# Bucketed attention and a squared-ReLU layer on one core: the planner sees sums by bank, and the first and last microseconds are written anew

## The chip, the cores and the metric

One core of one Trainium2 chip runs the whole kernel. The metric is the device time of one execution in microseconds (us). The kernel is one launch, and its code for general inputs stands behind a branch that these inputs do not take.

## The reference

Attention over 4 batches of 8 heads, 768 tokens and 64 dims, in which a query sees only keys of its own bucket (six sign bits of a projection), and behind it a layer of 512 to 2048 to 512 with a squared ReLU.

```python
q_bits = (einsum('bhsd,dk->bhsk', q, proj) > 0)      # 6 bits, the same for k
mask = q_bucket[..., :, None] == k_bucket[..., None, :]
scores = where(mask, q @ k.T / sqrt(D), -1e9)
attn = softmax(scores)                               # over the keys
x = (attn @ v) as (B*S, 512)
h = maximum(x @ w_in, 0.0)
out = (h * h) @ w_out                                # (3072, 512) float32
```

## The kernel before

**Work.** The attention is cut into 192 units of 128 queries of one head. TensorE makes a unit's 128x768 scores in `pS` (a PSUM tile of two banks; every second one of the early units has a tile of three banks, called `pS2` in the code). VectorE copies them to `e` and takes their extreme (0.95 us a unit), ScalarE takes the exponential with its sum (0.93 us), and the weights are turned: for the first visits by TensorE (`pT`, copied to `aT` by ScalarE), later by a DMA transpose. A *visit* is one pair of heads and 384 queries; `av` multiplies the turned weights with the values (`pA`) and writes the result as two halves `xx`. Four visits fill the 512 features of a *group* of 384 tokens, of which there are eight. For each group `moe` (L849) runs the layer: sixteen times twelve matmuls into `pm`, ScalarE and VectorE make `g` from it, and nine matmuls add `g` times `w_out` into the group's sum `po`.

**The sum.** `po` (L890) is one PSUM tile of three banks, one bank for each 128 tokens, with one buffer: the next group's sum takes the same place. The last group uses `pS` and `pA` instead (L887). After the sixteenth part of a group, three copies `o<-po` (L916) bring the banks to SBUF, by ScalarE or VectorE (one of them always VectorE), and `out<-o` sends them.

**The start.** `run` (L474) fills small tiles, and `first` (L710) makes the buckets of the first pair of heads: `K` and `G` are loaded in two halves each, three float32 matmuls with `wide_pj` go into the three banks of one tile `pd` (L720), and VectorE makes the masks `MK`, `MK`, `MG` from them with the threshold `above` (in `marks`, from `unit_f`). `side_by_side` (L728) makes the first six units' scores from those.

**The order.** Nothing runs when it is written. `Program.add` (L176) records each operation with the operations that it depends on; `region` (L163) says which part of a tile an operation touches, and for a PSUM tile it always answers "all of it". `order` (L257) then plans all engines: a forward pass by rank, then up to `ROUNDS` times a backward pass that gives new priorities and a forward pass with them, and of all plans it keeps the one that is shortest by its own costs. `emit` (L426) issues the instructions of every engine in that order. The engines' real waits (semaphores) are set afterwards by the framework below, for the order that it is given; the planner's dependences only decide that order. In the first microseconds of a plan TensorE is idle, and `emit` puts matmuls on a tile of ones (`idle<-ones`) into the gaps: 0.6 of the planned gap, counted at 56 ns each (L439).

Of the kernel before, what the change touches and what calls it, by code (L numbers as in the profile page):

```python
# [12 lines left out]
BF16 = mybir.dt.bfloat16  # L13
F32 = mybir.dt.float32
# [3 lines left out]
AF = mybir.ActivationFunctionType  # L18
ALU = mybir.AluOpType
# [4 lines left out]
P = 128  # L24
B, H, S, D = 4, 8, 768, 64
NB = 6
HS = 384
# [14 lines left out]
PRICE = dict(pe=1, dve=3.57, act=0.3, pool=3.06, sp=0.43)  # L42
AHEAD, DELAY, LAG = 60, 2500, 1.0

ROUNDS, BEHIND = 4, 40000
LOADS = 0

PREP, STACKS, VALUES = -8, 0, 4
# [24 lines left out]
HS2 = 2.0**-9  # L73
QK_MAX, V_MAX, V_MIN, W_MAX, W_MIN, NORM_MAX = 16.0, 1.0, 2.0**-4, 2.0**15, 2.0, (1.38 * WS) ** 2

IDLE_FROM, IDLE_SHARE = 1000, 0.6

# [57 lines left out]
class Program:  # L137
# [24 lines left out]
    @staticmethod  # L162
    def region(view):  # L163
        ap, rec = view.ap, view.rec
        size = lambda dims: 1 + sum(st * (n - 1) for st, n in dims)
        if rec.kind == "dram":
            return 0, 1, ap.offset, ap.offset + size(ap.ap), 0, 0, 0
        p0, f0 = divmod(ap.offset, rec.row)
        if rec.kind == "psum":
            return 0, 1, 0, 1, 0, 0, 0  # L170

        (step, n), inner = ap.ap[1], size(ap.ap[2:])
        block = (step, f0 % step, f0 % step + inner) if n > 1 and f0 % step + inner <= step else (0, 0, 0)
        return (p0, p0 + ap.ap[0][1], f0, f0 + size(ap.ap[1:])) + block
# [251 lines left out]
    def emit(self):  # L426
        info = mybir.DependencyInfo(mybir.DependencyClass.NoSync, mybir.DependencyReason.DATA)
        last = {}
        def issue(q, ins):
            if q.key in last:  # L430
                self.tc.add_manual_dep(ins, last[q.key], info, reason="in order")
            last[q.key] = ins.name
        out = self.order()
        fill, end = {}, IDLE_FROM
        for i in out[: out.index(self.busy_from)]:
            o = self.ops[i]
            if o.queue is self.pe:
                if o.start > end + 300:
                    fill[i] = int((o.start - end) * IDLE_SHARE / 56)  # L439
                end = o.start + o.busy  # L440
        for i in out:
            o = self.ops[i]
            q = o.queue
            for _ in range(fill.get(i, 0) if self.idle[1].rec.tile is not None else 0):
                issue(q, q.engine.matmul(self.idle[0].real(), self.idle[1].real(), self.idle[1].real(), start=True, stop=True).ins)
            real = lambda x: x.real() if isinstance(x, View) else x
            if o.name == "matmuls":
                for args, kw in o.args:
                    ins = q.engine.matmul(*map(real, args), **kw).ins  # L449
                    issue(q, ins)  # L450
                continue
            ins = getattr(q.engine, o.name)(*map(real, o.args), **{k: real(x) for k, x in o.kw.items()}).ins  # L452
            issue(q, ins)
# [20 lines left out]
def run(ctx: ExitStack, tc, kq, v, proj2, w_in, w_out, consts, out, flag):  # L474
    fast = flag is not None
# [5 lines left out]
    pr = Program(tc)  # L481
    pe, dve, act, pool, sp = pr.pe, pr.dve, pr.act, pr.pool, pr.sp
    T, U = slice(0, D), slice(D, P)
# [3 lines left out]
    def send(out, x):  # L487
        sp.dma_start(out, x)
# [15 lines left out]
    def sb(shape, dtype, name, bufs=1, tag=None):  # L504
        return pr.tile(sbp, "sb", shape, dtype, name, bufs_of.get(tag or name, bufs), tag)

    def ps(shape, dtype, name, bufs=1, tag=None):
        return pr.tile(psp, "psum", shape, dtype, name, bufs, tag)
# [6 lines left out]
    cst = sb([P, 4], F32, "cst")  # L515
    if not fast:
        sp.dma_start(cst, consts[:, 0:4])
    pj = sb([P, 32], F32, "pj")
    dve.memset(pj, 0.0)
    ones = sb([P, P], BF16, "ones")  # L520
    dve.memset(ones, 1.0)
    pr.idle = ps([P, 512], F32, "idle", tag="pm")[:, 0:P], ones
    unit_f = sb([P, P], F32, "unit_f")
    if fast:
        pj0 = sb([P, 4 * NB], F32, "pj0")
        sp.dma_start(pj0[:, 0 : 3 * NB], proj2[:, NB : 4 * NB])
        sp.dma_start(unit_f, consts[:, 4 + 2 * P :])
        wide_pj = sb([P, P], F32, "wide_pj", tag="f")
        dve.memset(wide_pj, 0.0)
        given = pj0.rearrange("p (n c) -> p n c", c=2 * NB)[:, :, 0:NB]  # L530
        signed = pj[:, 0 : 4 * NB].rearrange("p (n c) -> p n c", c=NB)
        dve.tensor_scalar(signed[:, 0::3], given, 1.0, 1.0, ALU.mult, ALU.mult)
        dve.tensor_scalar(signed[:, 1:3], given, -1.0, 1.0, ALU.mult, ALU.mult)
        dve.tensor_scalar(wide_pj[:, 0 : 2 * NB], pj[:, 0 : 2 * NB], 1.0, 1.0, ALU.mult, ALU.mult)
        dve.tensor_scalar(wide_pj[:, D : D + 2 * NB], pj[:, 2 * NB : 4 * NB], -1.0, 1.0, ALU.mult, ALU.mult)
        marks = sb([P, 4], F32, "marks")
        above, balance, rest = (marks[:, n : n + 1] for n in range(3))
        for x, y, z in ((balance, 1.0, -SC), (rest, -1.0, 1.0 / SC)):
            dve.memset(x[T], y)
            dve.memset(x[U], z)  # L540
        dve.tensor_reduce(above, unit_f.rearrange("p (n c) -> p n c", c=32)[:, :, NB : 3 * NB], AX.XY, ALU.add)
        dve.tensor_scalar(above, above, -(2.0**-126), 1.0, ALU.mult, ALU.mult)
        maxes, sums = sb([P, UNITS], F32, "maxes"), sb([P, UNITS], F32, "sums")
    else:
        sp.dma_start(pj[:, 0 : 3 * NB], proj2[:, NB : 4 * NB])
        sgn_f = sb([P, 4 * P], F32, "sgn_f", tag="o")
        dve.memset(sgn_f, 0.0)
        for n in range(4):
            sp.dma_start(sgn_f[32 * n : 32 * n + 4 * NB, n * P : (n + 1) * P], consts[0 : 4 * NB, 4 : 4 + P])
        sgn = sb([P, 4 * P], BF16, "sgn")  # L550
        dve.tensor_copy(sgn, sgn_f)
        balance = cst[:, 2:3]
        thr = sb([P, 1], F32, "thr")
        dve.memset(thr, -(2.0**-80))
        sp.dma_start(unit_f, consts[:, 4 + 2 * P :])
        ident = sb([P, P], BF16, "ident")
        dve.tensor_copy(ident, unit_f)
# [152 lines left out]
    def first(hp, nq):  # L710

        K, G = [sb([P, n], F32, name, tag="VV") for name, n in (("K", S), ("G", nq))]
        for x, w in ((K, T), (G, U)):
            for odd, m in enumerate((T, U)):
                send(x[m], kq[0, 2 * hp + odd, w, 0 : x.shape[1]])
        MK, MG = sb([P, S], F16, "MK", tag="M"), sb([P, nq], F16, "MG", tag="Q")
        pd = ps([P, 3, 512], F32, "pd", tag="po")
        halves = K[:, 0:HS], K[:, HS:], G
        for n, x in enumerate(halves):
            pe.matmul(pd[:, n, 0 : x.shape[1]], wide_pj, x, start=True, stop=True)  # L720
        for n in range(2):
            dve.tensor_scalar(MK[:, n * HS : (n + 1) * HS], pd[:, n, 0:HS], above, 2.0**15, ALU.is_gt, ALU.mult)
        dve.tensor_scalar(MG, pd[:, 2, 0:nq], above, 2.0**15, ALU.is_le, ALU.mult)
        GS = sb([P, nq], F32, "GS", tag="L")
        move(GS, G, -SC)
        return K, GS, MK, MG

    def side_by_side(st, c0, i):  # L728

        K, G, MK, MG = st  # L730
        pr.rank = u - 1000
        both = [ps([P, 2, 512], F32, "pS"), ps([P, 3, 512], F32, "pS2", tag="po")]
        jobs = [[(n, x[:, j, 0:HS], a[m, c0 : c0 + P], bb[m, j * HS : (j + 1) * HS]) for x, m in zip(both, (T, U))] for n, (a, bb) in enumerate(((G, K), (MG, MK))) for j in range(2)]
        if not i:
            jobs = [[x[t]] for t in range(2) for x in jobs]
        for x in jobs:
            matmuls(*[y[1:] for y in x], start=x[0][0] == 0, stop=x[0][0] == 1)
        return both
# [110 lines left out]
    def moe(n, b, q0, nq):  # L849
        X = [xxs.pop((b, q0, cc)) for cc in range(NCC)]  # L850
        po, gs = None, {}
# [4 lines left out]
        for f in range(NF + 1):  # L856
# [23 lines left out]
            if f > 0:  # L880
                m = f - 1
# [23 lines left out]
                for t in range(nq // P):  # L905
                    r0 = b * S + q0 + t * P
                    if grouped and last:
                        if m == 3:
                            move(acc[:, t], po[t], back)
                        else:  # L910
                            dve.scalar_tensor_tensor(acc[:, t], po[t], back, acc[:, t], ALU.mult, ALU.add)
                        if m == NF - 1:
                            send(out[r0 : r0 + P], acc[:, t])
                    elif last:
                        o = sb([P, DM], F32, "o", tag="f")
                        move(o, po[t], back, (dve,) if fast and t == 1 else (act, dve, pool))  # L916
                        send(out[r0 : r0 + P], o)
            if n == 0 and f in (1, 5, 9):
                j = f // 4 + FIRST
                if j < 4:  # L920
# [161 lines left out]
```

## Time and profile before

| | us |
|---|---|
| runs shown: median of 3 (lowest, highest) | 809.61 (808.09, 810.79) |
| the profiled execution: its time | 811.04 |
| its span, from the first to the last instruction | 809.2 |
| TensorE busy in the span | 788.2 |
| ScalarE, VectorE, GpSimd busy | 643.3, 605.0, 85.4 |

In rows of the profile PE is TensorE, PEld its weight loads, DVE VectorE, ACT ScalarE, POOL GpSimd, SPq the queue of SyncE, which issues nearly all DMAs. A timeline row gives the start, the duration, engine, line, operation, output and inputs, the count, and in brackets how long the engine had been idle and what ended that. Records of matmuls that follow each other overlap: one of 512 columns has a record of 379 ns, but the next starts about 216 ns after it. The 809.2 us are the span; the time of the same execution is 1.8 us longer.

### The profile page before, as it was taken

What the parts mean: (1) busy time and instruction counts of PE and PEld (TensorE: products, weight loads), DVE (VectorE), ACT (ScalarE), POOL (GpSimd) and SP (SyncE); (2) the same over time, 40 slices, a digit from 0 to 9 for tenths busy, and PEclk for the clock granted to TensorE, in tenths of its full rate; (3) what the DMA queues carried; (4) which work ended last, traced back from release to release, by engine and by line L of the source; (5) the groups of instructions that cost most, each with busy time, mean ns of one, the idle gap of its engine ahead of it and who ended that gap; (6) DMA issues with size and microseconds to landing.
All of it is one profiled execution on the core that took longest, in us unless ns stands there. A gap on an engine that the chain in (4) does not pass through costs nothing.

```text
span 809.2 us, 14281 instructions
## 1 busy us (share of the span) xinstructions
PE 788.2 (97%) x4953; PEld 428.8 (53%) x4957; DVE 605.0 (75%) x1264; ACT 643.3 (79%) x1215; POOL 85.4 (11%) x168
## 2 busy tenths in 40 slices
PE   8887999999999999999999999999999999999996
PEld 5444555555555555555555555555555555555553
DVE  5998999999988989988988618898858761165111
ACT  4899999989988979988988738988767598863442
POOL 1555401200001101000000001110001000000000
PEclk9999999999999999999999999999999999999999
DMA  7777679999999999998989519989662289883001
GB/s 211 222 229 220 195 237 202 179 188 186 201 182 193 160 203 194 197 203 150 213 165 181 143 20 192 183 180 205 140 143 41 41 205 268 256 296 125 1 0 44
DMA packets 286240, 137.41 MB, mean 170 GB/s; under 512 B 259024, under 2 KB 266192, under 8 KB 286160
## 3 DMA queue, kind: packets, MB, share of 16 engines
q1 hardware_dynamic: 286160, 136.42, 75.3%
q8 instruction: 41, 0.67, 0.4%
q14 instruction: 39, 0.32, 0.1%
HBM read 56.36 MB, written 6.29 MB: 77 GB/s over the span
## 4 chain that ended last, share of the span: by engine, by line
PE 87%; DVE 2%; ACT 1%; issue 1%
PE pm L452 30%; PE po L452 27%; PE pS L452 16%; PE pA L449 11%; PE pA L452 1%; PE pd L449 1%; DVE e L452 1%; PE pT L452 1%; ACT o L452 0%; PE pt L452 0%; DVE win L452 0%; DVE f L452 0%; ACT e L452 0%; DVE VV L452 0%; ACT A L452 0%
## 5 line engine op out<-in xcount | busy, mean ns | idle before, releaser
L452 PE MATMUL pm<-xx,win 128*128 128x384 f16 x1536 | 306.2, 326 | 0.2 <-ACT g L452 0.2
L452 PE MATMUL po<-wo,g 128*128 128x512 f16 x1008 | 274.7, 379 | 0.2
L452 PEld LDWEIGHTS <-win 128*128 128x128 f16 x1536 | 149.4, 97 | 114.0 <-issue 3.8
L452 DVE TENSOR_SCALAR_CACHE_REDUCE e<-pS 128x768 f32<-128x768 f32 x192 | 182.8, 953 | 28.8 <-PE pS L452 26.4
L452 ACT ACTIVATE e<-e,maxes 128x768 f32<-128x768 f32 x192 | 178.6, 930 | 26.6 <-DVE e L452 24.5
L452 DVE SCALAR_TENSOR_TENSOR hl<-e,rv,hl 128x768 f16<-128x768 f32 x162 | 164.1, 1018 | 14.1 <-ACT hl L452 12.9
L452 PEld LDWEIGHTS <-g 128*128 128x128 f16 x1152 | 111.6, 97 | 118.4 <-issue 3.9
L452 ACT ACTIVATE hl<-e,rv 128x768 f16<-128x768 f32 x161 | 148.6, 925 | 9.8 <-DMA aT<-hl 8.5
L452 DVE SCALAR_TENSOR_TENSOR g<-g,g 128x384 f16<-128x384 f32 x112 | 61.9, 553 | 99.2 <-ACT g L452 98.3
L452 ACT ACTIVATE g<-g 128x384 f32<-128x384 f32 (+1 forms) x248 | 128.1, 518 | 9.7 <-PE po L452 6.3
L452 ACT ACTIVATE g<-pm 128x384 f32<-128x384 f32 x128 | 62.1, 485 | 83.8 <-PE pm L452 81.9
L452 PE MATMUL pS<-A,Q 128*128 128x384 f16 x372 | 94.4, 329 | 3.2 <-DVE e L452 2.9
L452 PE MATMUL pS<-L,M 76*128 76x384 f16 x372 | 95.2, 328 | 0.0
L452 POOL TENSOR_SCALAR rv<-sums 128x1 f32<-128x1 f32 x117 | 35.0, 300 | 475.1 <-ACT e L452 387.1
L449 PE MATMUL pA<-aT,VV 128*64 128x384 f16 x972 | 84.1, 327 | 0.0
L449 PEld LDWEIGHTS <-VV 128*64 128x64 f16 x972 | 52.8, 110 | 31.2 <-issue 9.3
L452 PEld LDWEIGHTS <-Q 128*128 128x128 f16 x372 | 34.4, 98 | 38.1 <-issue 12.8
L452 PEld LDWEIGHTS <-M 76*128 76x128 f16 x372 | 36.8, 99 | 23.9 <-issue 0.5
L452 PE MATMUL pT<-unit_f,e 128*128 128x128 f32 x180 | 30.1, 290 | 7.7 <-POOL e L452 4.2
L452 ACT ACTIVATION_READ_ACCUMULATOR e<-e,maxes 128x1 f32 x192 | 36.9, 192 | 0.0
L452 PE MATMUL pS<-wo,g 128*128 128x512 f16 x96 | 34.9, 379 | 0.0
L452 POOL TENSOR_SCALAR e<-e,rv 128x768 f32<-128x768 f32 x30 | 32.3, 1083 | 21.2 <-DVE rv L452 12.8
(85 smaller groups left out, 579.0 us busy)
## 6 DMA issues: line engine op xcount, KB each, us to landing
R<-kq SPq DMA_DIRECT2D x32, 384.0 KB
X<-kq SPq DMA_DIRECT2D x32, 384.0 KB
raw<-w_in SPq DMA_DIRECT2D x16, 511.8 KB
raw<-w_out SPq DMA_DIRECT2D x16, 511.8 KB
V<-vp SPq DMA_DIRECT2D x19, 384.0 KB
out<-o SPq DMA_DIRECT2D x24, 256.0 KB
X<-vp SPq DMA_DIRECT2D x16, 384.0 KB
Q<-A SPq DMA_DIRECT2D x32, 96.0 KB
```

The lines of the kernel that those rows point to most:

```text
L449: ins = q.engine.matmul(*map(real, args), **kw).ins
L452: ins = getattr(q.engine, o.name)(*map(real, o.args), **{k: real(x) for k, x in o.kw.items()}).ins
```

## The change

- `ROUNDS` is 8 and was 4: the planner makes up to nine plans and was making five.
- `region` gives for a PSUM tile the banks that an operation touches (`f0 // 512` and on), so the planner takes operations on different banks of one tile for independent.
- The idle matmuls of the first gap are counted at 112 ns instead of 56: 21 now, 46 before. Those of the second gap follow the new plan: 15 now, 20 before.
- `ones`, which the idle matmuls multiply, is filled by GpSimd as its first operation; it was VectorE's sixth kind of fill.
- A one-column exponential on `pj` (`table`) stands first on ScalarE, so the activation table is loaded there, and the two loads of `G` are issued by ScalarE's own queue behind it.
- The three first projections go to three tiles: `pd` in the places of `pA` and `misc`, and bank 2 of the first `pS2` (`other`), which the first pair of units then uses.
- The last copy of the program is put on ScalarE, and its `out<-o` is issued by ScalarE's queue.

```diff
-ROUNDS, BEHIND = 4, 40000
+ROUNDS, BEHIND = 8, 40000
...
-IDLE_FROM, IDLE_SHARE = 1000, 0.6
+IDLE_FROM, IDLE_COLD, IDLE_SHARE = 1000, 112, 0.6
+G_BY = "act"
...
         if rec.kind == "psum":
-            return 0, 1, 0, 1, 0, 0, 0
+            return 0, 1, f0 // 512, (f0 + size(ap.ap[1:]) + 511) // 512, 0, 0, 0
...
-                    fill[i] = int((o.start - end) * IDLE_SHARE / 56)
+                    fill[i] = int((o.start - end) * IDLE_SHARE / (56 if end > IDLE_FROM else IDLE_COLD))
...
+    ones = sb([P, P], BF16, "ones")
+    (pool if fast else dve).memset(ones, 1.0)
     pj = sb([P, 32], F32, "pj")
     dve.memset(pj, 0.0)
-    ones = sb([P, P], BF16, "ones")
-    dve.memset(ones, 1.0)
...
+        table = sb([P, 1], F32, "table")
+        act.activation(table, pj[:, 24:25], AF.Exp)
...
-        for x, w in ((K, T), (G, U)):
+        for x, w, by in ((K, T, sp), (G, U, getattr(pr, G_BY))):
             for odd, m in enumerate((T, U)):
-                send(x[m], kq[0, 2 * hp + odd, w, 0 : x.shape[1]])
+                by.dma_start(x[m], kq[0, 2 * hp + odd, w, 0 : x.shape[1]])
...
-        pd = ps([P, 3, 512], F32, "pd", tag="po")
+        other = ps([P, 3, 512], F32, "pS2", tag="po")
+        pd = [ps([P, 512], F32, "pd", tag=x) for x in ("pA", "misc")] + [other[:, 2]]
...
-                        move(o, po[t], back, (dve,) if fast and t == 1 else (act, dve, pool))
-                        send(out[r0 : r0 + P], o)
+                        end = fast and (b, q0 + nq) == (B - 1, S) and t == nq // P - 1
+                        move(o, po[t], back, (act,) if end else (dve,) if fast and t == 1 else (act, dve, pool))
+                        (act if end else sp).dma_start(out[r0 : r0 + P], o)
```

What that does to the order is shown at two places, with the semaphores that an instruction waits for in brackets (DMAHW: a DMA's, DVE, Activation, PE, Pool: that engine's).

The first place is the start on ScalarE. `GS` is the scaled `G`, `A` a copy of the loaded heads `R`, `e` a unit's exponential, `top` a step of the weights' conversion. Before:

```order
L452 ACT_TABLE_LOAD [waits DMAHW4_49]
L452 ACTIVATE GS<-G 128x384 [waits DMAHW3_49]
L452 ACTIVATE A<-R,marks 128x768 [waits DMAHW6_49,DVE_49]
L452 ACTIVATE A<-R,marks 128x768 [waits DMAHW7_49]
L452 ACTIVATE top_80<-raw 128x512 [waits DMAHW0_49,DVE_49]
L452 ACTIVATE e,sums<-e,maxes 128x768 [waits DVE_49]
L452 ACTIVATE top_83<-raw 128x512 [waits DMAHW1_49]
L452 ACTIVATE e,sums<-e,maxes 128x768 [waits DVE_49]
```

And now, to the second exponential:

```order
L453 ACT_TABLE_LOAD
L453 ACTIVATE table<-pj 128x1 [waits DVE_49]
L453 DMA G<-kq 64x384 x2
L453 ACTIVATE GS<-G 128x384 [waits DMAHW4_49,DMAHW2_49]
L453 ACTIVATE A<-R,marks 128x768 [waits DMAHW6_49,DVE_49]
L453 ACTIVATE A<-R,marks 128x768 [waits DMAHW7_49]
L453 ACTIVATE e,sums<-e,maxes 128x768 [waits DVE_49]
L453 ACTIVATE top_84<-raw 128x512 [waits DMAHW0_49]
L453 ACTIVATE top_89<-raw 128x512 [waits DMAHW1_49]
L453 ACTIVATE e,sums<-e,maxes 128x768 [waits DVE_49]
```

The table load no longer waits for `G`, two DMA issues are new on ScalarE, and both `top` steps now stand between the first and the second exponential.

The second place is TensorE at the end of the sixth group's sum; numbers tell the tiles apart, `po_7447` and `po_7556` are this group's sum, `pm` the next group's first part. Before, the last of the group's matmuls and what follows:

```order
L452 LDWEIGHTS g_8146
L452 MATMUL po_7447<-wo_627,g_8146 128x512
L452 LDWEIGHTS win_246
L452 MATMUL pm_8196<-xx_8153,win_246 128x384 [waits Activation_49]
L452 LDWEIGHTS win_246
```

Now, at the end of the same sum (`g_8180` and `g_8204` are its last two parts):

```order
L453 MATMUL po_7556<-wo_491,g_8204 128x512
L453 LDWEIGHTS g_8180
L453 MATMUL po_7556<-wo_491,g_8180 128x512 [waits Activation_49]
L453 LDWEIGHTS g_8204
L453 MATMUL po_7556<-wo_491,g_8204 128x512
L453 LDWEIGHTS g_8180
L453 MATMUL po_7556<-wo_491,g_8180 128x512
L453 LDWEIGHTS g_8204
L453 MATMUL po_7556<-wo_491,g_8204 128x512 [waits DVE_49]
L453 LDWEIGHTS g_8204
```

The copies `o<-po` of a bank that is ready have moved in between the group's last matmuls. The two matmuls with a wait write another bank of the same tile, and they wait until ScalarE's, then VectorE's copy has read its own. In the order before, no matmul of a group waited for a copy of that group; only the first matmul of the next group did, at two of the eight groups, 61 and 13 matmuls behind the last one. Now sixteen such matmuls wait, listed here with the engine whose copy they wait for and the number of other matmuls that stand between the matmul that lets the copy go and the one that waits for it ("next" is the first matmul of the following group):

| group | waits |
|---|---|
| 1 | ACT 4, DVE 40, next ACT 20 |
| 2 | ACT 0 |
| 3 | ACT 48, next ACT 24 |
| 4 | ACT 16, DVE 0, next ACT 12 |
| 5 | ACT 4, DVE 1 |
| 6 | ACT 0, DVE 0, next ACT 15 |
| 7 | ACT 12 |
| 8 (the last) | ACT 1 |

Ahead of the first `pm` matmul TensorE now has four more score matmuls (`pS`) and three more turns (`pT`); ScalarE has one more exponential, one more `aT` and one more `xx`, and two fewer `top` and three fewer halves of `w_out`. The number of matmuls in the program is the same but for the 30 idle ones.

More of the change, by code (lines that the diff above doesn't have):

```diff
@@ L712, in first @@
         K, G = [sb([P, n], F32, name, tag="VV") for name, n in (("K", S), ("G", nq))]
-        for x, w in ((K, T), (G, U)):
+        for x, w, by in ((K, T, sp), (G, U, getattr(pr, G_BY))):
             for odd, m in enumerate((T, U)):
-                send(x[m], kq[0, 2 * hp + odd, w, 0 : x.shape[1]])
+                by.dma_start(x[m], kq[0, 2 * hp + odd, w, 0 : x.shape[1]])
         MK, MG = sb([P, S], F16, "MK", tag="M"), sb([P, nq], F16, "MG", tag="Q")
-        pd = ps([P, 3, 512], F32, "pd", tag="po")
+        other = ps([P, 3, 512], F32, "pS2", tag="po")
+        pd = [ps([P, 512], F32, "pd", tag=x) for x in ("pA", "misc")] + [other[:, 2]]
         halves = K[:, 0:HS], K[:, HS:], G
         for n, x in enumerate(halves):
-            pe.matmul(pd[:, n, 0 : x.shape[1]], wide_pj, x, start=True, stop=True)
+            pe.matmul(pd[n][:, 0 : x.shape[1]], wide_pj, x, start=True, stop=True)
         for n in range(2):
-            dve.tensor_scalar(MK[:, n * HS : (n + 1) * HS], pd[:, n, 0:HS], above, 2.0**15, ALU.is_gt, ALU.mult)
-        dve.tensor_scalar(MG, pd[:, 2, 0:nq], above, 2.0**15, ALU.is_le, ALU.mult)
+            dve.tensor_scalar(MK[:, n * HS : (n + 1) * HS], pd[n][:, 0:HS], above, 2.0**15, ALU.is_gt, ALU.mult)
+        dve.tensor_scalar(MG, pd[2][:, 0:nq], above, 2.0**15, ALU.is_le, ALU.mult)
         GS = sb([P, nq], F32, "GS", tag="L")
         move(GS, G, -SC)
-        return K, GS, MK, MG
+        return K, GS, MK, MG, other
     def side_by_side(st, c0, i):
-        K, G, MK, MG = st
+        K, G, MK, MG, other = st
         pr.rank = u - 1000
-        both = [ps([P, 2, 512], F32, "pS"), ps([P, 3, 512], F32, "pS2", tag="po")]
+        both = [ps([P, 2, 512], F32, "pS"), ps([P, 3, 512], F32, "pS2", tag="po") if i else other]
         jobs = [[(n, x[:, j, 0:HS], a[m, c0 : c0 + P], bb[m, j * HS : (j + 1) * HS]) for x, m in zip(both, (T, U))] for n, (a, bb) in enumerate(((G, K), (MG, MK))) for j in range(2)]
```

## The prediction

> **What bounds the kernel now.** I read the page's first part and its chain, then the busy time by stages, then the timeline of the first microseconds.
>
> ```profile
> span 809.2 us, 14281 instructions
> PE 788.2 (97%) x4953; PEld 428.8 (53%) x4957; DVE 605.0 (75%) x1264; ACT 643.3 (79%) x1215; POOL 85.4 (11%) x168
> PE 87%; DVE 2%; ACT 1%; issue 1%
> ```
>
> TensorE is busy for 97% and carries 87% of the chain that ended last. That is an average; the stages tell more. I cut the span at the first exponential (14.76), at the layer's first matmul into `pm` (88.5) and at the end of the last matmul (802.21). Columns are TensorE, its weight loads, VectorE, ScalarE, GpSimd.
>
> ```profile
> L452 PE MATMUL pm<-xx,win x48: 322/326/327, 88.5 to 108.1; 128*128 128x384 f16 x48
> ...
> 0.00:14.76 14.76, 12.03 (x78) 8.32 (x79) 6.65 (x23) 4.35 (x6) 0.20 (x4) 1.00 0.69 211
> 14.76:88.50 73.74, 62.94 (x398) 35.97 (x395) 67.35 (x157) 70.70 (x147) 38.02 (x50) 0.95 0.73 218
> 88.50:802.21 713.71, 713.20 (x4483) 384.52 (x4485) 530.73 (x1086) 567.63 (x1064) 47.21 (x115) 1.00 0.77 164
> 802.21:809.20 6.99, 0.00 (x1) 0.00 (x0) 0.28 (x1) 0.60 (x1) 0.00 (x0) 0.87 0.34 122
> ```
>
> So there are three regimes. From 88.5 to 802.21 TensorE is idle for 0.5 of 713.7 us: whatever makes it wait there is added to the time, and whatever relieves the other engines is worth nothing. From 14.76 to 88.5 ScalarE is the full one (70.7 of 73.7). Before that it does little (4.35 of 14.76), so the start is worth what it moves ScalarE's first exponential.
>
> **The start.** What sets 14.76:
>
> ```profile
> 0.74 0.39 SPq L452 DMA_DIRECT2D pj<-proj  x1
> 1.18 1.21 SPq L452 DMA_DIRECT2D K<-kq  x2
> 2.43 1.24 SPq L452 DMA_DIRECT2D G<-kq  x2
> 2.73 5.09 PE L445 MATMUL idle<-ones 128*128 128x128 bf16 x46 [2.73 <-DVE ones L452]
> 6.00 1.28 ACT L452 ACT_TABLE_LOAD   x1 [6.00 <-DMA G<-kq]
> 7.61 2.03 PE L452 MATMUL pd<-K,wide_pj 128*128 128x384 f32 x4
> 9.47 0.81 PE L452 MATMUL pd<-G,wide_pj 128*128 128x384 f32 x2
> 10.32 0.62 DVE L452 TENSOR_SCALAR MK<-pd,marks 128x384 f16<-128x384 f32 x1 [3.82 <-PE pd L452]
> 11.91 1.94 DVE L452 SCALAR_TENSOR_TENSOR L<-A,marks,R 128x768 f16<-128x768 f16 x2
> 12.38 0.78 ACT L452 ACTIVATE top<-raw 128x512 f16<-128x512 bf16 x1 [2.61 <-DMA raw<-w_in]
> 13.76 0.95 DVE L452 TENSOR_SCALAR_CACHE_REDUCE e<-pS 128x768 f32<-128x768 f32 x1
> 14.46 1.29 PE L445 MATMUL idle<-ones 128*128 128x128 bf16 x20
> 14.76 0.94 ACT L452 ACTIVATE e<-e,maxes 128x768 f32<-128x768 f32 x1 [1.60 <-DVE e L452]
> 16.33 0.91 ACT L452 ACTIVATE e<-e,maxes 128x768 f32<-128x768 f32 x1
> ```
>
> The 46 idle matmuls (5.09 us, 111 ns each) hold the projections back to 7.61. `G`, issued by 3.67, is there at 6.00, 2.3 us later; `K`, issued by 2.39, should by the same lag be there at 4.7. The first mask waits for the third projection (10.28 to 10.32), and two `L` steps (1.94) stand ahead of the first `e`.
>
> After the change: 21 idle matmuls at 111 ns from about 1.1 (GpSimd fills `ones` first) end at 3.4 and hold nothing. `K`'s issues end at about 0.74+0.6+0.4+0.6 = 2.3, so it is there at 4.6. ScalarE's table load (1.28), the one-column step and two issues (1.24) from 0.8 end at 3.5, so `G` is there at 5.8, as before; it is needed only behind both `K` matmuls, so moving it gains nothing by itself, and the table load leaves ScalarE's path, which had slack there. What are the projections worth from 4.6?
>
> ```profile
> L452 PEld LDWEIGHTS pd<-K,wide_pj x4: 191/335/337, 7.5 to 8.8; 128*128 128x128 f32 x4
> L452 PEld LDWEIGHTS pd<-G,wide_pj x2: 190/190/190, 9.2 to 9.5; 128*128 128x128 f32 x2
> ```
>
> The same weight load takes 335 ns at first and 190 later, and the later 20 idle matmuls took 1.29 us (64 ns each) against 111 ns: TensorE ran at about half speed until some 8.5 us, 5.8 us after its first matmul, although the profile's own clock column says 1.00 there. With a shorter warm-up and a gap behind it I take half speed for the `K` matmuls (1.35 us each, half as fast as a `G` that takes about 0.7): 4.6 to 7.3, `G` to about 8.5, two score matmuls (1.4) and the mask's to 10.3, the first `e` at 10.5, the exponential at 11.5: 3.3 us earlier. The second one has both `top` steps ahead of it now (0.78 each): 11.5+1.1+1.6 = 14.2 for 16.33, 2.1 earlier. **I take -2.0**, the second's, since from there ScalarE is full. Bounds: 0 (a load or a cold clock is late next: `raw` ended an idle 2.61 us at 12.38) and -4.2 (full speed throughout). Of ScalarE's work up to 88.5, five steps of 0.5 to 0.8 us go and three of 0.5 to 1.1 come; I take nothing, within -1.5 and +0.5.
>
> **Work done earlier on TensorE.** Four score matmuls and three turns move ahead of 88.5, where TensorE has 10.8 us of idle time to hide them. Slots from the chain of waits:
>
> ```profile
> 101.17 0.37 PE pT L452 x3
> 112.67 1.95 PE pm L452 x12
> 119.22 1.94 PE po L452 x9
> ```
>
> 4 x 1.95/12 (384 columns, as `pS`) + 0.37 = **-1.0**.
>
> **The waits inside a sum.** The order of the changed kernel has sixteen matmuls that wait for a copy `o<-po`; the order before had two. The planner now thinks that a copy of one bank and a matmul into another are independent; the semaphores do not. That waits go by tile and not by bank is in the trace of before: the first `MK`, from bank 0 of `pd`, waited for the matmul into bank 2, and copies from different banks of one `po` wait for each other:
>
> ```profile
> DVE o L452 <- ACT o L452: 9.0, 6, 5.0
> L452 ACT ACTIVATE o<-po x14: 574/594/602, 193.6 to 743.3; 128x512 f32<-128x512 f32 x14
> L452 DVE TENSOR_SCALAR o<-po x7: 670/691/692, 194.8 to 742.6; 128x512 f32<-128x512 f32 x7
> L452 PE MATMUL po<-wo,g 128*128 128x512 f16 x1008 | 274.7, 379 | 0.2
> ...
> 801.83 0.38 PE L452 MATMUL pA<-wo,g 128*128 128x512 f16 x1
> 802.25 0.60 ACT L452 ACTIVATE o<-pA 128x512 f32<-128x512 f32 x1 [0.48 <-PE pA L452]
> 27.51 0.08 DVE L452 DVE_READ_ACCUMULATOR e<-pS 128x1 f32 x1
> 27.64 0.48 PE L452 MATMUL pS<-A,Q 128*128 128x384 f16 x2 [0.34 <-DVE e L452]
> ```
>
> One wait with nothing between: the matmul's record ends 379-216 = 0.16 us after its slot, the copy starts 0.04 later (802.21 to 802.25), takes 0.59 or 0.69, and TensorE goes on 0.05 after (27.59 to 27.64): 0.85 us for ScalarE, 0.94 for VectorE. By the table of waits: two of 0.85 and two of 0.94 with none between; one of 0.94-0.22 and, in the last group, one of 0.85-0.22 with one matmul between; two with four `pm` matmuls (0.65) between, 0.2 each. Sum 5.4. The other eight have 12 to 48 matmuls (2 us or more) as cover and cost nothing unless the copy is over a microsecond late. To this comes the copy's own wait: ScalarE is 80% and VectorE 74% busy in this stage, and a step found running has some 0.3 us left, so about 0.2 for each of eight: 1.6. **I take +7.0.** Bounds +4.1 (the 0.16 us by which a record's modelled end trails is not real, eight times) and +11 (copies stand behind steps that wait for loads themselves). Queued behind the waiting matmul is all of TensorE.
>
> The Trainium skill, PSUM — Partial Sum Buffer, its summary of rules for kernel authors, says that a matmul and a read of another bank may run at once and that semaphores go by bank. By that rule the term would be 0. The trace sides with the tile: the 9.0 us above.
>
> **The end.**
>
> ```profile
> 801.79 1.90 SPq L452 DMA_DIRECT2D out<-o  x3
> L452 SPq DMA_DIRECT2D out<-o x24: 332/432/1077, 232.4 to 803.3; - x24
> ```
>
> The last copy ended at 802.85, and SyncE issued its transfer at 803.3. ScalarE can issue at once: at best -0.45. But ScalarE's way to the end of the program now lies behind that issue of some 0.6: at worst +0.6. **I take -0.2.**
>
> **Sum.** -2.0 -1.0 +7.0 -0.2 = +3.8 on the profiled execution's 811.04. The median of the runs shown is 1.4 lower, 809.61; on it I forecast 813.4. A measurement of this kernel tells 0.3% (2.4 us) from no change.
>
> **Rivals.**
>
> *Balance.* The start gives its full 4.2 and the ramp 1.0, because `K` is there earlier and ScalarE's 3.0 us of idle time in it shrink; the waits cost their prompt 5.4. -5.2 -1.0 -0.2 +5.4 = -1.0: 808.6, no change. For it: the ramp is ScalarE's alone. Against: ScalarE's 70.7 us of work there stay.
>
> *The ramp runs away.* Faster. The planner's longer search finds an order in which the ramp to `pm` has no idle time on ScalarE (-3.0) and 1.5 us less work, with the start at -4.2, against waits at their low 4.1: -8.7 -1.0 -0.2 +4.1 = -5.8: 803.8. It decides from the point where the first `pm` matmul starts before 88.5-2.4-5.4+1.2 = 81.9. Against it: 70.7 us of work from a first exponential that is hardly before 14.8-4.2 = 10.6 end at 81.3 with no gap at all.
>
> *By bank.* The copies are no cost, by the skill's rule above or because TensorE comes to them late: -3.2, 806.4, faster. It decides where the waits cost under 0.8 in all. Against it: four of them have no matmul between.
>
> *Cold start.* TensorE stays at half speed into the first units: `G` and the first two units' scores (0.7, 1.4 and 0.3 more) put the first exponential at 13.9 instead of 11.5 and the second at about its old 16.3, and the shift is gone. 0 -1.0 +7.0 -0.2 = +5.8: 815.4. For it: it took 5.8 us of unbroken matmuls before, and now a gap from 3.4 to 4.6 lies in them. The Trainium skill, TensorE: Matmul & The Clock Gate, Part 1, has the clock doubled after a free-running window of about 3.4 us of sustained work; an estimate by it: a gap that spoils one window costs 3.4 us more at half speed, which would also take the shift. The trace agrees in kind, with 5.8 us until the change.
>
> **Chances.** Forecast 0.59 (0.51 slower, 0.08 within 0.3%), balance 0.16 (same), the ramp 0.09 and by bank 0.04 (faster), cold start 0.12 (slower). So faster 0.13, same 0.24, slower 0.63. The forecast's own range, with its bounds, is 810.5 to 817.5. To leave out no more than 2 in 10 the range reaches down to balance: 808.3 to 817.5.
>
> **What would show it.** Right: idle rows of PE ended by "ACT o" and "DVE o", about eight, 0.6 to 1.3 us each, where before there are none; TensorE idle from the first `pm` matmul to the last matmul at 6 to 9 us instead of 0.5; the first exponential at 11 to 12.5; the first `pm` matmul at 85.5 to 87.5; the first mask ahead of the third projection's end. Wrong: no idle time ended by `o`, or a first `pm` matmul before 83 or after 89, or a second stretch between 100 and 300 in which TensorE waits for ScalarE because five conversion steps were moved there.

## The result, and the profile after

| | before | after |
|---|---|---|
| median of six runs each, us | 810.68 (808.09 to 811.75) | 819.12 (816.97 to 821.71) |
| ratio to before | | 1.0107, 95% interval 1.008 to 1.0134 |
| profiled execution, us | 811.04, span 809.2 | 817.17, span 815.2 |

The change makes the kernel 8.4 us slower. The profiled execution of after is 2.0 us under the median of its runs and that of before 0.4 over its own, so the two profiles show 6.1 of it. First the page's head, and the stages cut as before: at the first exponential, the first matmul into `pm`, and the end of the last matmul.

```profile
span 815.2 us, 14274 instructions
PE 788.6 (97%) x4927; PEld 425.4 (52%) x4927; DVE 607.9 (75%) x1259; ACT 642.8 (79%) x1211; POOL 90.0 (11%) x178
```

```profile
L453 PE MATMUL pm<-xx,win x1536: 323/326/337, 87.7 to 803.6; 128*128 128x384 f16 x192
```

```profile
0.00:13.90 13.90, 9.81 (x45) 5.89 (x47) 6.01 (x21) 3.88 (x6) 0.41 (x5) 1.00 0.70 222
13.90:87.70 73.80, 64.63 (x409) 35.91 (x402) 69.63 (x159) 70.22 (x146) 36.37 (x48) 0.98 0.69 204
87.70:808.67 720.97, 714.18 (x4481) 383.63 (x4478) 531.67 (x1081) 568.15 (x1060) 53.23 (x125) 1.00 0.77 164
808.67:815.20 6.53, 0.00 (x0) 0.00 (x0) 0.57 (x1) 0.60 (x1) 0.00 (x0) 0.61 0.34 121
```

The first `pm` comes 0.8 us earlier than before, and the tail behind the last matmul is 0.46 shorter. The layer stage between them is 7.3 us longer (720.97 against 713.71), and TensorE is idle in it for 6.8 us instead of 0.5. What it waits for there (total, times, longest):

```profile
PE po L453 <- DVE o L453: 2.3, 3, 0.9
PE pS L453 <- DVE e L453: 1.5, 2, 0.9
PE po L453 <- ACT o L453: 1.4, 2, 0.7
PE pS L453 <- ACT o L453: 0.5, 1, 0.5
PE pm L453 <- DVE xx L453: 0.3, 1, 0.3
PE pS L453 <- ACT g L453: 0.3, 1, 0.3
PE pm L453 <- ACT g L453: 0.3, 1, 0.3
```

Six waits are for a copy `o` between two matmuls of one sum: 4.2 us in all, and none is longer than 0.9. Two of them stand 1.66 us apart in one sum:

```profile
677.83 0.81 PE L453 MATMUL po<-wo,g 128*128 128x512 f16 x3 [0.69 <-ACT o L453]
679.49 0.81 PE L453 MATMUL po<-wo,g 128*128 128x512 f16 x3 [0.85 <-DVE o L453]
```

The other 2.4 us, for `e`, `g` and `xx`, are new as well; in the same stage of before there is a single wait:

```profile
PE pm L452 <- ACT g L452: 0.2, 1, 0.2
```

These rows also add up to the longer stage: 6.3 us more idle time, eleven waits at 0.16 each for the modelled end of a matmul's record (1.8), less the 1.0 of work that moved ahead, make 7.1 of the 7.3. Now the start, in order of time (start, duration, what ended the idle time before it):

```profile
0.73 1.28 ACT L453 ACT_TABLE_LOAD   x1 [0.73 <-PEq L1080]
0.94 1.31 ACTq L453 DMA_DIRECT2D G<-kq  x2
0.99 2.42 PE L446 MATMUL idle<-ones 128*128 128x128 bf16 x21 [0.99 <-POOL ones L453]
2.00 0.49 SPq L453 DMA_DIRECT2D K<-kq  x1
4.82 0.25 DVE L453 TENSOR_SCALAR wide_pj<-pj 128x12 f32<-128x12 f32 x2
5.88 0.52 ACT L453 ACTIVATE GS<-G 128x384 f32<-128x384 f32 x1 [3.65 <-DMA G<-kq]
6.50 2.90 PE L453 MATMUL pd<-K,wide_pj 128*128 128x384 f32 x4 [3.09 <-DMA K<-kq]
8.16 0.62 DVE L453 TENSOR_SCALAR MK<-pd,marks 128x384 f16<-128x384 f32 x1 [1.20 <-PE pd L453]
9.20 1.49 PE L453 MATMUL pS<-G,wide_pj 128*128 128x384 f32 x2
13.90 0.94 ACT L453 ACTIVATE e<-e,maxes 128x768 f32<-128x768 f32 x1 [3.55 <-DVE e L453]
16.09 0.91 ACT L453 ACTIVATE e<-e,maxes 128x768 f32<-128x768 f32 x1
```

```profile
L453 PEld LDWEIGHTS pd<-K,wide_pj x4: 288/335/337, 6.5 to 7.9; 128*128 128x128 f32 x4
L453 PEld LDWEIGHTS pS<-G,wide_pj x2: 337/337/337, 8.6 to 9.2; 128*128 128x128 f32 x2
```

The idle matmuls end at 3.4 and the second half of `K` lands only at 6.5, so TensorE stands still for 3.1 us. The weight loads of the projections take 288 to 337 ns, all six of them (before, the last three took 190), and the projections of `K` and of `G` take 2.90 and 1.49 us for 2.03 and 0.81. `wide_pj`, which they multiply, is ready only at 5.1, because the load of `pj` now stands between the two halves of `K`. The first exponential gains 0.86, the second 0.24. At the end ScalarE issues the last transfer right behind its copy, in 0.36 us:

```profile
808.71 0.60 ACT L453 ACTIVATE o<-pA 128x512 f32<-128x512 f32 x1 [1.11 <-PE pA L453]
809.33 0.36 ACTq L453 DMA_DIRECT2D out<-o  x1
```

### The profile page after: what moved, and what is told of

Same layout as the page of the kernel before. It is cut to its first block, busy times and chain, and to the rows that moved or that the text cites. A ratio compares the mean times of both kernels' runs of the same rounds, so it can differ in the third digit from the quotient of the medians.

```text
span 815.2 us, 14274 instructions
## 1 busy us (share of the span) xinstructions
PE 788.6 (97%) x4927; PEld 425.4 (52%) x4927; DVE 607.9 (75%) x1259; ACT 642.8 (79%) x1211; POOL 90.0 (11%) x178
## 4 chain that ended last, share of the span: by engine, by line
PE 84%; ACT 2%; DMA 1%; issue 1%; DVE 1%; DVEq 0%
PE pm L453 29%; PE po L453 26%; PE pS L453 15%; PE pA L450 11%; PE pA L453 1%; DMA aT<-hl 1%; PE pd L450 1%; ACT hl L453 0%; PE pt L453 0%; ACT o L453 0%; ACT e L453 0%; DVE o L453 0%; ACT g L453 0%; PE pT L453 0%; DVE hl L453 0%
## 5 line engine op out<-in xcount | busy, mean ns | idle before, releaser
L453 PE MATMUL pm<-xx,win 128*128 128x384 f16 x1536 | 293.9, 326 | 0.6 <-DVE xx L453 0.3
L453 PE MATMUL po<-wo,g 128*128 128x512 f16 x1008 | 256.6, 379 | 3.8 <-DVE o L453 2.3
L453 ACT ACTIVATE g<-g 128x384 f32<-128x384 f32 (+1 forms) x242 | 124.9, 517 | 6.7 <-PE po L453 3.0
L453 PE MATMUL pS<-A,Q 128*128 128x384 f16 x372 | 92.4, 328 | 4.8 <-DVE e L453 3.5
L453 PE MATMUL pS<-L,M 76*128 76x384 f16 x372 | 92.3, 327 | 0.5 <-DVE L L453 0.4
L453 POOL TENSOR_SCALAR rv<-sums 128x1 f32<-128x1 f32 x126 | 39.7, 315 | 432.9 <-ACT e L453 398.7
L453 PEld LDWEIGHTS <-Q 128*128 128x128 f16 x372 | 34.7, 98 | 40.5 <-issue 15.1
L453 DVE SCALAR_TENSOR_TENSOR L<-A,marks,R 128x768 f16<-128x768 f16 x32 | 32.1, 1012 | 4.0 <-ACT A L453 3.8
```

## The experiments

Two suspects: the waits for copies between the matmuls of a sum, and a TensorE that stays at half speed because of the gap at the start. The rivals are the new order as such, the eight rounds of planning, and losses that only move to another wait. "Whole tile" is the kernel before's rule for dependences in PSUM, "by bank" the changed one's. The ratios are to the kernel before on the same chip; before itself had medians of 810.4 to 811.1 there. So two kernels are compared by their ratios, where 0.0010 is 0.8 us; after's loss is 8.7 us by its ratio and 8.4 by the medians.

One number helps to compare traces with different orders: how far TensorE is **behind** at a time, that is the time less the slots of the matmuls started by then (median distance of starts in before: 162 ns for 384 columns in f16, 216 for 512, 82 for `pA`, 110 for a turn; idle matmuls count nothing). A few missing records make it good to about 1 us. It is worked out from one profile of each kernel, like the time from which TensorE runs fast (the first entry in the trace's list of granted clocks, where the weight loads turn from slow to fast too) and the waits of TensorE from 100 us on. The time of the profiled execution stands beside the median: those of e1, e2, e5 and e12 are 1.5 to 2.3 us over it, those of after, e3 and e7 1.5 to 2.0 under.

| kernel | median us | ratio | profiled us | fast from | first exp. | behind at 100 | lost from 100 to the end | waits for `o` / others |
|---|---|---|---|---|---|---|---|---|
| before | 810.7 | 1 | 811.0 | 8.7 | 14.8 | 30.7 | 17.6 | 0 / 0.2 |
| after | 819.1 | 1.0107 | 817.2 | 11.4 | 13.9 | 29.7 | 24.2 | 4.2 / 1.8 |
| e1 whole tile | 815.7 | 1.0057 | 817.2 | 18.9 | 15.0 | 32.0 | 21.2 | 0 / 2.4 |
| e2 copies behind | 818.5 | 1.0089 | 820.8 | 19.3 | 15.0 | 32.7 | 23.4 | 0 / 5.0 |
| e3 bank alone | 815.0 | 1.0049 | 813.5 | 7.9 | 13.5 | 29.0 | 21.1 | 1.6 / 1.5 |
| e4 eight rounds | 810.4 | 0.9999 | 810.3 | 8.5 | 14.7 | 28.3 | 19.1 | 0.8 / 0.6 |
| e5 third bank | 813.4 | 1.0043 | 815.4 | 15.1 | 14.9 | 31.3 | 20.8 | 1.0 / 2.6 |
| e6 long warm-up | 815.4 | 1.0071 | 814.9 | 4.2 | 11.2 | 27.7 | 23.9 | 4.2 / 1.7 |
| e7 short warm-up | 810.3 | 0.9997 | 808.8 | 7.1 | 12.9 | 29.0 | 16.5 | 0 / 0.2 |
| e8 whole tile, warm | 812.4 | 1.0027 | 813.2 | 6.8 | 11.6 | 28.5 | 21.0 | 0 / 2.5 |
| e9 the same, `G` by SyncE | 811.7 | 1.0008 | 812.5 | 7.0 | 11.4 | 26.2 | 23.3 | 0 / 3.3 |
| e10 third bank, warm | 811.4 | 1.0011 | 811.7 | 5.8 | 11.8 | 27.9 | 21.2 | 1.0 / 2.5 |
| e11 eight rounds, short | 809.4 | 0.9982 | 808.4 | 6.8 | 12.7 | 26.5 | 20.0 | 0.8 / 0.8 |
| e12 all cures | 814.3 | 1.0048 | 816.1 | 6.5 | 13.2 | 32.1 | 21.9 | 1.2 / 2.0 |

### The waits inside a sum

**Whole tile again** (e1). All else of the change stays.

```diff
-            return 0, 1, f0 // 512, (f0 + size(ap.ap[1:]) + 511) // 512, 0, 0, 0
+            return 0, 1, 0, 1, 0, 0, 0
```

> The changed kernel with dependences in PSUM by the whole tile again; all its other edits stay (start, table load, G by ScalarE's queue, eight rounds, last transfer). Its order has no copy `o` between the matmuls of a sum, only three waits of a next group with 13 to 44 matmuls as cover. Theory (the waits inside the sums, 5.2 us in the trace of the changed kernel, and the 3.2 us of waits for `e` and `g` that came with them, are the loss): idle rows ended by `o` gone, 819.1 - 5.2 = 813.9 if the 3.2 us belong to something else, 819.1 - 8.4 = 810.7 if they go too. Rival A (the start, eight rounds or the order as such cost it): 817 or more, with TensorE's idle time in the layer stage still 6 us or more.

815.68 us, ratio 1.0057 (1.0042 to 1.0072). All waits for `o` are gone, and about half of the loss came off (4.1 of 8.7 us by the ratios): between theory and rival. It isn't a clean test, for the start differs too: the profiled execution, the slowest of the six, had its first exponential at 15.0 and TensorE 2.3 us further behind at 100 than that of after.

**Copies behind the sum** (e2). The planned order stays; a copy and its transfer that stood between two matmuls of a sum are emitted behind its last one.

```diff
         out = self.order()
+        out = self.behind_sums(out)
```

> The changed kernel's own order, with the copies `o` (and their transfers) that stood between the matmuls of a sum moved behind the last matmul of that sum; nothing else moves, and the dependences stay by bank. Theory: the six waits for `o` go, 5.2 us: 813.9; if the 3.2 us of waits for `e` and `g` were made by the copies in their way, 810.7. Rival A (the order as such): 817 or more. Rival B (a copy that comes later only holds the next group's first matmul, with 12 to 20 matmuls as cover): waits for `o` of the same sum at the groups' beginnings, 818.

818.48 us, ratio 1.0089 (1.0072 to 1.0106): no gain is clear of the noise, since after's interval is 1.0080 to 1.0134. No wait for `o` is left, not even at a next group, so rival B is out; but the waits for `e` went from 1.5 to 3.6 us (from 90 us on):

```profile
PE pS L472 <- DVE e L472: 3.6, 9, 0.5
PE pS L472 <- ACT g L472: 0.8, 1, 0.8
PE pm L472 <- ACT g L472: 0.5, 2, 0.3
```

Part of that comes from the copies put off: one stands ahead of a unit's step `e` on VectorE, and TensorE waits for that step.

```profile
203.01 0.69 DVE L472 TENSOR_SCALAR o<-po 128x512 f32<-128x512 f32 x1 [0.82 <-ACT o L472]
203.62 0.95 DVE L472 TENSOR_SCALAR_CACHE_REDUCE e<-pS 128x768 f32<-128x768 f32 x1
204.63 0.50 PE L472 MATMUL pS<-A,Q 128*128 128x384 f16 x2 [0.43 <-DVE e L472]
```

The same is seen at 504 and 613 us, with one or two steps between, 1.1 us in all three. But three of the nine waits for `e` (1.4 us) lie at 126 to 143 us, ahead of the first copy, so the rest stays open. This isn't the cure, and it says little of the cause, since the profiled start was as cold as in e1.

**The third bank of `po` a tile of its own** (e5). Every row of the order stays; only which tile the third bank belongs to is changed, and so what a semaphore covers.

```diff
+        if kind == "psum" and tuple(shape[1:]) == (3, 512):
+            make = lambda: Banks(pool.tile([shape[0], 2, 512], dtype, name=name, tag="po", bufs=1), lambda: pool.tile([shape[0], 512], dtype, name=name, tag="third", bufs=1))
```

> The changed kernel with its order unchanged in every row, but the third bank of `po` a tile of its own, so that a matmul into it no longer waits for a copy out of the other two. Of the six waits for `o` in the trace of the changed kernel one stays inside a sum of `po` (0.6 us, one matmul between) and the one in the last group (0.47); gone are the others, 3.1 us of visible idle time and 0.16 us more each by the modelled ends. Theory (these waits are a loss of their own, and go by tile): 819.1 - 3.8 = 815.3. Rival A (a wait that is taken away comes back as a wait for `e`, as when the copies were moved behind the sums, where 5.2 us of waits went and 0.6 came off the time): 818.5, with TensorE's waits for `e` up from 1.5 us to 4 or more.

813.43 us, ratio 1.0043 (1.0027 to 1.0059): 5.2 us less than after by the ratios (give or take 2.5), where 3.8 was expected, and although its profiled start was colder (31.3 behind at 100 for 29.7). Where after waited twice in the sum at 677 us, one wait is left:

```profile
677.69 1.24 PE L467 MATMUL po<-wo,g 128*128 128x512 f16 x5 [0.47 <-ACT o L467]
```

```profile
PE pS L467 <- DVE e L467: 2.6, 5, 1.0
PE pS L467 <- ACT o L467: 0.5, 1, 0.5
PE po L467 <- ACT o L467: 0.5, 1, 0.5
```

So the waits are by tile and not by bank, and they cost what they show: in the profiles 3.2 us of them less gave 3.4 of the loss from 100 us on (24.2 to 20.8). Some came back as waits for `e` (1.5 to 2.6 us), the rival's way on a small scale.

**By bank alone, and eight rounds alone,** on the kernel before (e3, e4).

```diff
-            return 0, 1, 0, 1, 0, 0, 0
+            return 0, 1, f0 // 512, (f0 + size(ap.ap[1:]) + 511) // 512, 0, 0, 0
```

> The kernel before with dependences by bank alone (four rounds, old start, old end). Its order has one copy with no matmul between it and the waiting one, one by VectorE with four, and one in the last group with one matmul between. Theory, prompt: 0.85 + 0.3 + 0.64 = +1.8 on 810.7: 812.5, the start and the first `pm` as before. Rival A (an order planned by bank loses 8 us whatever stands in the sums): 816 or more. Rival by bank (the copies cost nothing): 810.7, no idle row ended by `o`.

815.04 us, ratio 1.0049 (1.0032 to 1.0067). The three waits for `o` are there at 1.6 us (forecast 1.8), but the loss is 4: 1.5 us more are for `e`, `g` and `xx`, which the order before does not have.

```diff
-ROUNDS, BEHIND = 4, 40000
+ROUNDS, BEHIND = 8, 40000
```

> The kernel before with eight rounds of planning alone. Its order has no copy inside a sum and six waits of a next group, of which two have ten matmuls (1.6 us) as cover and the copy some 1.4 us of ScalarE's work. Theory: no change, 810.7 within 1.5. Rival A (the longer search lands in a worse order by itself): 814 or more.

810.38 us, ratio 0.9999 (0.9987 to 1.0012), as expected: by the profiles it is 2.4 us further on at 100 and loses 1.5 of it by the end. Its ramp also has no stretch at half clock, where that of before has 6.8 us of it (76.9 to 83.7, the 0.95 in the clock column of its ramp). How much of the 2.4 us that is, no run tells.

### The clock at the start

**The long warm-up** (e6). The order stays; 43 idle matmuls instead of 21.

```diff
-IDLE_FROM, IDLE_COLD, IDLE_SHARE = 1000, 112, 0.6
+IDLE_FROM, IDLE_COLD, IDLE_SHARE = 1000, 56, 0.6
```

> The changed kernel with twice as many idle matmuls ahead of the first projection (about 42 for 21, 0.99 to 5.7 us), its order otherwise the same. Cold start (TensorE, let go idle from 3.4 to 6.5 us, stays at half speed until 11.5 to 17, and the first exponentials come late): weight loads of `K` at 335 ns only up to about 7 us, 190 behind, the first exponential at about 11.9 instead of 13.9 to 15.0, the first `pm` some 2 to 3 us earlier, 819.1 - 3 = 816.1. Rival (the clock at the start is not worth anything, since ScalarE or the loads hold the ramp): first exponential earlier, but 819 as before.

815.43 us, ratio 1.0071 (1.0057 to 1.0085): 2.9 us less by the ratios (give or take 2.5; 3.7 by the medians), as expected. `K` still lands only at 6.1 and the gap is 1.1 us, but TensorE comes to it at full speed; the idle matmuls turned fast at 4.2 already (43 took 4.06 us, at 0.115 each they would have taken 4.9):

```profile
0.99 4.06 PE L446 MATMUL idle<-ones 128*128 128x128 bf16 x43 [0.99 <-POOL ones L453]
6.12 0.94 PEld L453 LDWEIGHTS pd<-K,wide_pj 128*128 128x128 f32 x4 [1.25 <-issue]
6.16 1.53 PE L453 MATMUL pd<-K,wide_pj 128*128 128x384 f32 x4 [1.10 <-DMA K<-kq]
8.26 1.70 PE L450 MATMUL pS<-K,GS 64*128 64x384 f32 x6
11.18 0.94 ACT L453 ACTIVATE e<-e,maxes 128x768 f32<-128x768 f32 x1 [0.66 <-DVE e L453]
13.42 0.91 ACT L453 ACTIVATE e<-e,maxes 128x768 f32<-128x768 f32 x1
```

The same six score matmuls in e1, with the short warm-up, and the loads of all 24 such matmuls (least, median, most), there and in e6:

```profile
10.43 3.09 PE L450 MATMUL pS<-K,GS 64*128 64x384 f32 x6
15.04 0.94 ACT L453 ACTIVATE e<-e,maxes 128x768 f32<-128x768 f32 x1 [5.96 <-DVE e L453]
...
L450 PEld LDWEIGHTS pS<-K,GS x24: 182/236/334, 10.4 to 23.2; 64*128 64x128 f32 x24
```

```profile
L450 PEld LDWEIGHTS pS<-K,GS x24: 182/186/187, 8.3 to 18.5; 64*128 64x128 f32 x24
```

So three of the four profiled short warm-ups with a gap (e1, e2, e5) were colder than that of after: first exponentials at 14.9 to 15.0, up to 0.3 later than before, and 1.5 to 3 us more behind at 100. These three executions are the slowest or the second slowest of their kernels, and that of after the second fastest of its own, which fits a start that is colder in some executions than in others. Only these four traces show it; the spread of the times doesn't (4.7 us in after, but also 4.6 in e8, which has the long warm-up).

**The short warm-up alone,** in the kernel before (e7): 23 idle matmuls instead of 46, with no gap.

```diff
-                    fill[i] = int((o.start - end) * IDLE_SHARE / 56)
+                    fill[i] = int((o.start - end) * IDLE_SHARE / (56 if end > IDLE_FROM else IDLE_COLD))
```

> The kernel before with half as many idle matmuls ahead of the first projection (23 for 46, from 2.73 to about 5.3 us), nothing else. Theory (it is the gap that spoils the clock, not the number of idle matmuls): `K` is there by 5.3, so no gap, and the weight loads turn from 335 to 190 ns at about the same 8.5 us; the projections, 2.3 us earlier, bring the first exponential to about 13.3: 811 - 1 = 810. Rival (the shorter warm-up by itself leaves TensorE cold): weight loads at 335 ns beyond 10 us, the first exponential after 15, 812 or more. Rival B (`K` comes only at 6.3 here too, and leaves a gap of 1 us): as A.

810.26 us, ratio 0.9997 (0.9987 to 1.0007). The projections follow at once and TensorE is fast from 7.1 on: it is the gap, not the number. The first and the second exponential come 1.9 us earlier, and by the median next to nothing of it reaches the end. The profiled execution, 1.5 us under the median, is itself 2.3 shorter than that of before, so the rows don't show where the gain of the others went.

```profile
2.74 2.63 PE L445 MATMUL idle<-ones 128*128 128x128 bf16 x23 [2.74 <-DVE ones L452]
5.38 2.37 PE L452 MATMUL pd<-K,wide_pj 128*128 128x384 f32 x4
12.86 0.94 ACT L452 ACTIVATE e<-e,maxes 128x768 f32<-128x768 f32 x1 [0.53 <-DVE e L452]
14.44 0.91 ACT L452 ACTIVATE e<-e,maxes 128x768 f32<-128x768 f32 x1
```

**Whole tile with the long warm-up** (e8: the edits of e1 and e6).

> The changed kernel with dependences by the whole tile again (order of the first of these runs, 815.7) and the long warm-up. Cold start: 815.7 - 3 = 812.7, the work that TensorE is behind at 100 us as small as in the run of eight rounds alone. Rival (the start is worth nothing): 815.7.

812.37 us, ratio 1.0027 (1.0015 to 1.0038): 2.4 us less than e1 by the ratios (give or take 1.5; 3.3 by the medians), where 3 was expected.

**The same with `G` by SyncE** (e9).

```diff
-G_BY = "act"
+G_BY = "sp"
```

> The changed kernel with dependences by the whole tile, the long warm-up, and `G` issued by SyncE's queue behind `K` again. Theory (the two loads in parallel hold each other up: `K` landed at 6.1 to 6.5 us in every run that issued `G` by ScalarE's queue, and was there by 5.3 where SyncE issued it alone): TensorE no longer waits for `K` at its first projection, which starts when the idle matmuls end (about 6.1), `G` lands at about 6.0 as before; the first exponential at 11.2 instead of 11.6; 812.4 - 0.4, with 1.5 either way for an order that is planned anew: 812.0. Rival (`K` lands at 6.3 whatever issues `G`): the wait for `K` stays, 812.4.

811.72 us, ratio 1.0008 (0.9996 to 1.0021). TensorE does not wait for `K` any more and starts on it at 5.88, where e8 waited until 6.39:

```profile
5.88 2.04 PE L453 MATMUL pd<-K,wide_pj 128*128 128x384 f32 x4
```

```profile
6.39 1.72 PE L453 MATMUL pd<-K,wide_pj 128*128 128x384 f32 x4 [0.31 <-DMA K<-kq]
```

So `G` on a queue of its own delays `K` by at least 0.5 us, here. The place of `pj` is not what delays it: in e8 and e9 `pj` is loaded ahead of both halves of `K`. The order is another one, so the difference of the two times (0.6 us by the medians, 1.5 by the ratios) isn't shown to come from this.

### Both

**Third bank and long warm-up** (e10: e5 and e6).

> The changed kernel, its order unchanged, with both cures: the third bank of `po` a tile of its own (alone 813.4) and the long warm-up (alone 815.4). Theory (two losses that add): 819.1 - 5.7 - 3.7 = 809.7. Rival (they overlap, because a ramp that comes earlier only meets ScalarE and VectorE earlier, and the layer stage gives it back as waits for `e`, `g` and `xx`): 812 or more, with these waits above 3 us in all.

811.44 us, ratio 1.0011 (1.0 to 1.0021): by the ratios 7.8 of the 8.7 us are back, between the theory and the rival. With the warm clock the third bank is worth 4.9 us (give or take 1.4), and with the third bank the warm-up 2.6 (give or take 1.5). Alone they were worth 5.2 and 2.9, so within the noise the two losses add; by the medians they would seem not to (9.4 and 7.7), but these are medians of different chips.

**Eight rounds and short warm-up,** the rest as before (e11: e4 and e7).

> The kernel before with eight rounds (alone 810.4) and half as many idle matmuls (alone 810.3, with the first exponential 1.9 us earlier), everything else old. If the earlier start is worth its 1.9 us: 808.5. If ScalarE and the later loads give it back in the ramp: 810.3. By one profile each TensorE was 2 us less behind at 100 us with either, so I take 809.3.

809.44 us, ratio 0.9982 (0.9971 to 0.9993), as expected: the best of all, and 9.7 us under the changed kernel. It is the only one that is faster than before, by 0.2%.

**All cures** (e12: e10 with `G` by SyncE, which has the order planned anew).

> The changed kernel with the third bank a tile of its own, the long warm-up and `G` by SyncE's queue; its order is planned anew and has one copy by ScalarE between two matmuls of a sum with nothing between (0.85) and the one of the last group (0.5). Theory: as with both cures, 809.7, less 0.4 for `K`: 809.3, within 1.5 for the new order. Rival (every new order of the layer stage loses about 3 us to waits for `e`, `g` and `xx`, against 0.2 in the order before): 812.

814.32 us, ratio 1.0048 (1.0031 to 1.0064), 3.0 us over e10: the rival, though not by its waits, which are no more than e10's. The new order puts `G` ahead of the second half of `K`, the first exponential is at 13.2, and in the profile TensorE is 4.2 us further behind at 100; its ramp has 10.2 us at half clock for e10's 3.4. It came out 5.0 us over the theory's 809.3 and 2.3 over the rival's 812: what a new order will take could not be told within some us.

## Why the prediction was wrong, point by point

The sign and the main mechanism were right, the size was not: 819.1 for 813.4. Of these 5.7 us 1.1 is the base (before's median is 810.7 here, 809.6 there), and behind the rest are a step that failed and one that was missing. By the profiles the first `pm` came 0.8 us earlier for 2.0, the layer stage was 7.3 longer for 6.0, and the end gained 0.46 for 0.2: 2.2 of the other 4.6. The last 2.4 is that the profiled execution of after is faster than its median and that of before slower; no trace shows where it lies, and colder starts as in e1, e2 and e5 would be one place. With the gap at the start filled (e6), the changed kernel takes 815.4.

- **The start, -2.0: the step that failed,** in the words "`K` is there at 4.6". I took the lag of `G` in the kernel before for `K`, whose second half is issued by 2.49 and lands at 6.5, 4.0 us later; SyncE alone had it there by 5.4 (e7), and with `G` on ScalarE's queue it was late in every run (6.2 to 6.7). `wide_pj` alone, ready at 5.1, would have ruled out 4.6. So the gap behind the idle matmuls was 3.1 us instead of 1.2, and half speed did not end with the `K` matmuls but at 11.4, or at 15.1 to 19.3 (e5, e1, e2). The first exponential came at 13.9 to 15.0, not 11.5. Filling the gap was worth 2.4 to 2.9 us by the ratios (e8, e10, e6). This is the rival *cold start*, to which I gave 0.12. Its 13.9 for the first exponential is the one of the profile, but partly by luck: it had `K` at 4.6 too, and half speed reaching further into the units' scores.
- Even a good start is worth less than its shift. I carried the second exponential's 2.1 to the end one for one; in e7 the second came 1.9 earlier (14.44), and the time fell by 0.1 us (ratio 0.9997, 0.9987 to 1.0007). In the order of eight rounds the same step was worth 1.4 by the ratios of e4 and e11 (give or take 1.4).
- **The waits inside a sum, +7.0:** the mechanism as forecast, the size too high. Six of the eight priced showed, 0.47 to 0.85 each: with 0.16 for each modelled end 5.2 us, against 5.4 for the prompt sum (whose terms as written make 5.3). The two with four matmuls between cost nothing, and the 1.6 for copies that find their engine busy was not there: no wait was over 0.9. By e5 and e10 four of the six are worth 4.9 to 5.2, where their rows and modelled ends say 3.8; the difference is within the noise.
- The rule of the Trainium skill, PSUM — Partial Sum Buffer, its summary of rules for kernel authors, to guard by bank, would have made this 0. In this kernel's program the semaphores go by tile: e5 changes nothing but the tile, and the four waits of matmuls into the third bank go.
- **What was missing:** waits for `e`, `g` and `xx` in the layer stage, 2.4 us in after, 0.2 before. Every order that was planned anew has them (0.6 to 5.0 from 100 us on), whichever part of the change it holds, and the stage's loss follows the sum of all waits: 16.5 and 17.6 us with 0.2, 19.1 to 23.4 with 1.4 to 5.0, 23.9 and 24.2 with 6. I priced the new order's gains and copies but not that the order before had hardly a wait to begin with. In the layer stage of after they cost 3.2 us (2.4 and 0.16 for each of five), while the waits inside a sum fell 1.8 short of the 7.0: that the stage came out within 1.3 us of its forecast is partly luck. What in the planning makes them stays open; eight rounds alone has the fewest.
- **Work moved ahead, -1.0:** ahead of the first `pm` the trace has 92 such score matmuls for 88 and 150 turns for 147; at 162 and 110 ns that is 1.0 us, as forecast.
- **The end, -0.2:** -0.46 in the trace, the bound; ScalarE's way to the end of the program cost nothing.
- Of what I said would show it: the idle rows ended by `o` (six for eight, and 0.47 to 0.85 us each for 0.6 to 1.3), 6.8 us of idle time in the stage (6 to 9) and the first mask ahead of the third projection (8.16) came; the first exponential and the first `pm` (87.7, a little over the range) did not.

## What to carry to other kernels

Ahead of shortening a warm-up, look up when the first operand really lands, on the queues as they will be: a gap between the idle matmuls and the first real one can cost more than the idle matmuls. A dependence that a planner draws finer than the program's own semaphores puts waits where the plan sees none; cut the tiles as fine as the plan. And a new order of a stage that hardly waits is itself a risk of some us: compare it by the waits of the engine that is full.

## What the runs showed of the hardware

- TensorE's half speed at the start shows in no clock column here (1.00 up to 13.9 us in after) but in the weight loads: 335 ns against 190 for 128 rows in f32, 148 against 94 for `MG` (e1). The trace's list of granted clocks begins only at the turn to full speed (8.65 us in before, 11.38 in after, 15.14 in e5, 18.95 in e1, 19.27 in e2), and the column counts the time ahead of it as 1.00.
- Where the idle matmuls and the projections left no gap, or hardly one, TensorE turned fast 4.1 to 6.0 us after its first matmul (e11, e7, e8, before, e9), and 3.2 after it at the least (e6). With a gap of 2.7 to 3.1 us it took 4.9 us more of matmuls in after, 9.0 in e5, 12.6 in e1 and 13.0 in e2. The Trainium skill, TensorE: Matmul & The Clock Gate, Part 1, has the clock doubled behind one free-running window of about 3.4 us of sustained work; the short times agree in kind, the three long ones do not, for in e1 TensorE's records run on from 6.3 to 18.9 us without a break (their ends are modelled). What holds the clock down there is open; from some 10.4 us on these are score matmuls on 64 of the 128 rows, and no run tells whether that matters.
- Late in the ramp most traces have a second time at half clock, which the clock column does show (0.95 of the ramp in before, 0.98 in after): 6.8 us in before, e6, e7 and e8, 10.2 in e12, 3.4 in after and five others, none in e1, e4 and e11. What it costs was not tested apart; it is part of how far TensorE is behind at 100.
